# Late routing of a top-1 expert layer taken in steps inside the second products, its marks on VectorE, and the first rows' norms ahead of their transposes

## The chip, the cores and the metric

The kernel runs on one core of a Trainium2 chip. TensorE (PE) multiplies, its weight loads (PEld) overlap its products; VectorE (DVE), ScalarE (ACT) and GpSimd (POOL) compute, SyncE (SP) issues most of the transfers. The metric is the device time of one execution in microseconds; shorter is better. Three runs of the kernel before took 612.71, 613.78 and 613.82 us, median 613.78.

## What is computed

A linear attention with a norm for each head, and behind it a layer of 8 experts, of which each token goes through the one with the highest score.

```python
kv = np.einsum('bhsd,bhse->bhde', k, v)              # 8 batches, 8 heads, 576 tokens, 64
out = np.einsum('bhsd,bhde->bhse', q, kv)
rms = np.sqrt(np.mean(out * out, axis=-1, keepdims=True) + 1e-06)
x = rows_of(out / rms * g_norm)                      # 4608 tokens x 512
logits = x @ w_gate                                  # 8 experts
e_idx = np.argmax(logits, axis=1)
gate_w = softmax(logits)[np.arange(N), e_idx]
eom = 1 / (1 + np.exp(-(x @ w_output_gate)))
for e in range(8):
    mask = e_idx == e
    h = np.maximum(x[mask] @ w1[e], 0)               # 512 -> 1024
    out[mask] = gate_w[mask, None] * eom[mask, e, None] * (h @ w2[e])   # -> 512
```

## The kernel before, in words

**Early part.** `early()` goes through the first batches: `kv_part` makes the keys-values product of a batch in PSUM (`kvps`), a copy of it (`kvc`, L445, VectorE; `aug`, L446, ScalarE) is transposed and multiplied by the gate weights. `out_tile(g)` makes 128 rows of the attention (`ops`), writes them, unscaled, to a table in HBM (`xs`), and keeps squares and gate scores. The 36 tiles of 128 tokens are four groups of 10, 6, 10 and 10. For each group `route(gi)`, a generator, does the routing, nearly all of it on VectorE: the norms by a root iteration (L554 to L576, `xtail`), the scaling of the scores (L583), their sums and maximum (L587 to L600), the choice of expert (L604 to L613, `ohb`), the sums of the gates (L622 to L638); then TensorE counts each token's slot (`rps`, L641 to L650), VectorE reads it (L656 to L666), and `low` makes a 128x128 mark for each tile (`la`, L692). VectorE makes the table's right side (`rrc`, L702 to L709), writes the tail of each row (L713, L715, an SP transfer `xs<-xtail`), TensorE multiplies marks and right side (`tblps`, L724), and VectorE adds the result to `tacc` (L727, L729). The string in `PLACES` for a group says which engine makes which mark, V for VectorE and P for GpSimd, in turn.

**Order of routing.** A generator yields 0 between small operations and 1 at a pause. `advance()` takes every generator in `routing` to its next pause. `run_out` calls it after each tile, early and late; the loops at the end of `early()` and `late()` call it until nothing is left. `constant` and `constants(n)` issue 4n products of ones whose result nobody reads (L417, `cps`), called fillers below.

**Experts.** When the first 16 tiles (`EARLY`) are routed, `gather(0)` reads the first 256 rows of expert 0 with two indirect GpSimd transfers (L236, `xg`), and then `run(i)` works on one block of rows at a time: runs 0 to 7 are 256 rows of each expert, runs 8 to 15 the rest. A weight chunk (`wraw`, loaded by SP, L191) is split into two parts: ScalarE rounds it (`whi`, L211 and L218), VectorE takes the rest (`wlo`, L214 and L221). `stage(i, k)` transposes 128 gathered rows on TensorE (`tps`, L264, two PSUM buffers that are shared with `kvps`, `rps` and `tblps`) and splits them (`xT`, L267 ScalarE, L268 VectorE). `scale_heads` multiplies rows by their norms (L244): on GpSimd in `scale_rows` for every run but the first, for run 0 on VectorE inside `stage`.

The first products of a run are eight steps f of 12 products (`hps`, L289) in two PSUM buffers; of each, ScalarE makes the relu (L297) and VectorE its low part (L299, "relu half" below), after which the buffer is free for step f + 2. The second products are, for each of T tiles (T is 2 in runs 0 to 7), eight steps f of 3 products (`yps`, L326). `put(k, f, ...)` places an event behind step f of tile k: the splits of the next run's first weights, loads, the two `stage` calls of the next run and one `unit` per tile. In runs 0 to 6 a `unit` is one step of `late()`, which does the other batches, the tiles 16 to 35 and the routing of the last two groups; one unit also follows each step f of the first products. Engine orders are those of the code (`manual_schedule`): every engine executes in the order in which the instructions are issued there, and a waiting instruction holds all behind it.

## Time and profile before

| | |
|---|---|
| median of 3 runs | 613.78 us (612.71 to 613.82) |
| the profiled execution | 614.2 us, of which span 612.4 us |
| PE busy | 556.8 us (91%) |
| PEld busy | 484.0 us (79%) |
| DVE busy | 338.2 us (55%) |
| ACT busy | 285.7 us (47%) |
| POOL busy | 156.8 us (26%) |
| mean granted TensorE clock | 0.963 |

The busy shares are means over a part of some 90 us in front of run 0, a part of 240 us (runs 0 to 7, with late work beside them in runs 0 to 5), and the rest. What a stage waits for is read from the stage: from a table of busy time by stretch, from TensorE's timeline with the idle time in brackets ahead of an instruction, and from the engine that the bracket names as releaser. Times are counted from the start of the span.

### The profile page before, as it was taken

How to read it: one execution, taken by the hardware profiler on the slowest of the kernel's cores; microseconds unless marked ns; L12 is line 12 of the kernel's file. 1: busy time of each engine (PE TensorE's matmuls, PEld its weight loads, DVE VectorE, ACT ScalarE, POOL GpSimd, SP SyncE). 2: the span in 40 equal slices, each digit the busy share in tenths (PEclk: the TensorE clock that was granted, in tenths of full speed). 3: DMA queues.
4: the chain of work that ended last, by engine and by line, in shares of the span. 5: the costliest groups of instructions: out<-in, count | busy, mean ns of one | idle time of the engine just before them, and what ended most of it. 6: DMA issues, size and time to landing. Idle time of an engine off the chain costs nothing.

```text
span 612.4 us, 12185 instructions
## 1 busy us (share of the span) xinstructions
PE 556.8 (91%) x4829; PEld 484.0 (79%) x4829; DVE 338.2 (55%) x666; ACT 285.7 (47%) x481; POOL 156.8 (26%) x149
## 2 busy tenths in 40 slices
PE   7777749999999798999989999999999999999991
PEld 5656539888888687889878989889897988888980
DVE  2127846646586967765596535535445354656530
ACT  1445316658376434564544433435345453545420
POOL 2000340030301424323435216032331506050110
PEclk9989859999999988999999999999999999999996
DMA  8998966988765745776847426354453646464100
GB/s 310 406 405 329 328 235 220 371 256 311 234 244 200 246 155 161 241 210 202 276 157 238 129 103 209 121 162 165 151 185 125 218 145 207 141 217 137 42 19 17
DMA packets 43163, 125.96 MB, mean 206 GB/s; under 512 B 10302, under 2 KB 10430, under 8 KB 43104
## 3 DMA queue, kind: packets, MB, share of 16 engines
q1 hardware_dynamic: 35920, 105.19, 50.6%
q0 software_dynamic: 6752, 19.75, 9.6%
q8 instruction: 39, 0.64, 0.4%
q10 hardware_dynamic: 432, 0.22, 0.1%
q14 instruction: 20, 0.16, 0.1%
HBM read 105.94 MB, written 19.75 MB: 205 GB/s over the span
## 4 chain that ended last, share of the span: by engine, by line
PE 70%; issue 11%; DVE 6%; DMA 6%; ACT 3%; POOL 2%; another core or an unknown queue 1%; ACTq 0%; POOLq 0%; SPq 0%; DVEq 0%
PE yps L326 30%; PE hps L289 27%; PE ops L513 4%; PE tps L264 3%; PE kvps L438 3%; DMA ld<-qT 2%; DVE wlo L221 2%; DMA xg<-xs,gidx 1%; PE yps L320 1%; DMA wgs<-wg 1%; POOL out L338 1%; PE cps L417 1%; ACT whi L218 1%; DVE hT L299 1%; DMA xs<-xrow 1%
## 5 line engine op out<-in xcount | busy, mean ns | idle before, releaser
L289 PE MATMUL hps<-xT,whi 128*128 128x256 f32 (+8 forms) x1024 | 222.4, 309 | 10.1 <-DVE hT L299 8.8
L326 PE MATMUL yps<-whi,hT 128*128 128x512 f32 (+3 forms) x592 | 200.3, 402 | 0.0
L289 PEld LDWEIGHTS hps<-xT,whi 128*128 128x128 f32 x1024 | 170.7, 191 | 16.9 <-DVE hT L299 11.0
L289 PE MATMUL hps<-xT,wlo 128*128 128x256 f32 (+8 forms) x512 | 156.2, 305 | 0.0
L326 PEld LDWEIGHTS yps<-whi,hT 128*128 128x128 f32 (+3 forms) x592 | 110.8, 187 | 24.7
L338 POOL DMA_INDIRECT out<-y,oidx x42 | 45.1, 1075 | 318.0 <-ACT y L337 290.8
L299 DVE SCALAR_TENSOR_TENSOR hT<-hps,hT 128x256 fp32r<-128x256 f32 (+9 forms) x168 | 62.9, 395 | 102.8 <-ACT hT L297 94.9
L326 PE MATMUL yps<-wlo,hT 128*128 128x512 f32 (+3 forms) x296 | 116.5, 394 | 0.0
L297 ACT ACTIVATE hT<-hps 128x256 fp32r<-128x256 f32 (+8 forms) x128 | 55.4, 433 | 118.7 <-PE hps L289 113.5
L214 DVE SCALAR_TENSOR_TENSOR wlo<-wraw,gcol,whi 128x1024 fp32r<-128x1024 f32 x64 | 82.0, 1286 | 47.4 <-ACT whi L211 47.4
L289 PEld LDWEIGHTS hps<-xT,wlo 128*128 128x128 f32 x512 | 98.1, 192 | 0.3
L221 DVE TENSOR_TENSOR wlo<-wraw,whi 128x1024 fp32r<-128x1024 f32 x64 | 83.4, 1303 | 24.1 <-ACT whi L218 22.8
L211 ACT ACTIVATE whi<-wraw,gcol 128x1024 fp32r<-128x1024 f32 x64 | 72.9, 1149 | 0.0
L218 ACT CAST whi<-wraw 128x1024 fp32r<-128x1024 f32 x64 | 66.7, 1042 | 0.0
L326 PEld LDWEIGHTS yps<-wlo,hT 128*128 128x128 f32 (+3 forms) x296 | 55.6, 188 | 10.7
L244 POOL TENSOR_TENSOR xg<-xg 128x512 f32<-128x512 f32 (+8 forms) x40 | 49.4, 1240 | 33.8 <-DMA xg<-xs,gidx 32.8
L337 ACT ACTIVATE y<-yps,tl 128x512 f32<-128x512 f32 (+3 forms) x37 | 25.4, 688 | 66.5 <-PE yps L326 54.6
L236 POOL DMA_INDIRECT xg<-xs,gidx x42 | 47.0, 1118 | 16.2 <-issue 10.9
L267 ACT CAST xT<-tps 128x512 fp32r<-128x512 f32 (+8 forms) x42 | 23.0, 548 | 54.9 <-PE tps L264 53.9
L513 PE MATMUL ops<-aug,ld 64*64 64x80 f32 x1152 | 29.5, 238 | 11.1 <-DMA ld<-qT 5.1
L268 DVE TENSOR_TENSOR xT<-tps,xT 128x512 fp32r<-128x512 f32 (+8 forms) x42 | 26.7, 636 | 21.7 <-ACT xT L267 21.7
L518 ACT COPY xrow<-ops 128x512 f32<-128x512 f32 x36 | 21.3, 591 | 37.1 <-PE ops L513 28.9
(148 smaller groups left out, 405.9 us busy)
## 6 DMA issues: line engine op xcount, KB each, us to landing
wraw<-w SPq DMA_DIRECT2D x128, 512.0 KB, 4.4
ld<-kvm SPq DMA_DIRECT2D x32, 512.0 KB, 8.4
ld<-qT SPq DMA_DIRECT2D x18, 512.0 KB, 10.3
xs<-xrow SPq DMA_DIRECT2D x18, 512.0 KB, 3.6
ld<-rem SPq DMA_DIRECT2D x4, 512.0 KB, 7.5
xg<-xs,gidx POOLq DMA_INDIRECT x42
out<-y,oidx POOLq DMA_INDIRECT x42
xs<-xtail SPq DMA_DIRECT2D x3, 80.0 KB, 4.9
```

The costliest lines, as they stand in the source:

```text
L211: he.activation(hi, r, AF.Copy, scale=gcol[:, 0:1])
L214: eng.scalar_tensor_tensor(out=lo, in0=r, scalar=gcol[:, 0:1], in1=hi.bitcast(F32), op0=ALU.mult, op1=ALU.subtract)
L218: he.copy(hi, r)
L221: eng.tensor_tensor(out=lo, in0=r, in1=hi.bitcast(F32), op=ALU.subtract)
L236: nc.gpsimd.indirect_dma_start(out=x[:M, :], out_offset=None, in_=rows, in_offset=bass.IndirectOffsetOnAxis(ap=gidx[i // E][:M, p, t:t + 1 ...
L244: eng.tensor_tensor(out=v, in0=v, in1=f, op=ALU.mult)
L289: nc.tensor.matmul(ps[:, :C], w[:, o:o + P], x[d][:, :C], start=(d == 0 and k == 0), stop=(d == 3 and k == 2))
L297: nc.scalar.activation(h[:, 0:C], ps[:, :C], AF.Relu)
L299: nc.vector.scalar_tensor_tensor(out=h[:, l:l + b - a], in0=ps[:, a:b], scalar=0.0, in1=h[:, a:b].bitcast(F32), op0=ALU.max, op1=ALU.subtract)
L326: nc.tensor.matmul(ps[:M], a, b, start=(f == 0 and n == 0), stop=(f == 7 and n == 2))
L338: i_ = nc.gpsimd.indirect_dma_start(out=out, out_offset=bass.IndirectOffsetOnAxis(ap=oidx[i // E][:M, RUNS[i][0], t:t + 1], axis=0), in_=y ...
L513: nc.tensor.matmul(ps[c0:c0 + D, u, p * W:(p + 1) * W], qt[g // 2][r, p, q0:q0 + D], augs[b % 3][r, p, :], start=True, stop=True)
```

## The change

Five edits. `advance()` is called in `run_out` only while the first 16 tiles are made. A new `step(n)` takes only the oldest generator, through at most six small operations or to its next pause; the end of `late()` calls it in place of `advance()`, and in runs 0 to 7 it stands four times in each tile of the second products, behind f = 1, 3, 6 and 7. The marks of the last two groups are all made by VectorE (`PLACES`). For run 0 both tiles are scaled ahead of both `stage` calls, and 16 fillers stand in front of the first transposes, 4 in front of the second.

```diff
--- before.py
+++ after.py
@@ -64,7 +64,7 @@
 
 APART = (1, 2, 3)
 
-PLACES = ['PV', 'VVP', 'PV', 'PV']
+PLACES = ['PV', 'VVP', 'V', 'V']
 
 COLD = (2, 20, 4)
 
@@ -250,8 +250,6 @@
     def stage(i, k):
         t, c0, M = tiles_of(i)[k]
         x = xg.pop((i, t))
-        if i == 0:
-            scale_heads(x[:M], nc.vector)
         if k == 0:
             w = i // E
             n = (ROWS_A, CMAX)[w]
@@ -765,6 +763,16 @@
                 if k == 2:
                     routing.remove(r)
 
+    def step(n=6):
+
+        while n and routing:
+            n -= 1
+            k = next(routing[0], 2)
+            if k == 2:
+                routing.pop(0)
+            if k:
+                break
+
     def run_out(limit):
         nonlocal done_tiles
         if done_tiles < limit:
@@ -772,7 +780,8 @@
             done_tiles += 1
             if len(squares) > 2:
                 sums()
-            advance()
+            if done_tiles <= EARLY:
+                advance()
             return True
         return False
 
@@ -866,7 +875,7 @@
             sums()
             yield
         while routing:
-            advance()
+            step()
             yield
 
     vec = nc.vector
@@ -1029,8 +1038,11 @@
         for x in range(Tn):
             put(*places[x * len(places) // Tn], stage, i + 1, x)
         if i < E:
+
             for k in range(T):
                 put(k, 3, unit, 8 + k)
+                for f in (1, 3, 6, 7):
+                    put(k, f, step)
         order = list(range(T))
         if last_run and half(i):
             order.insert(1, order.pop())
@@ -1048,6 +1060,9 @@
         ps_y[0] = main.enter_context(tc.tile_pool(name="ps_y", bufs=1, space=psum))
         split(0, 1, 0)
         for k in range(TA):
+            scale_heads(xg[(0, k)], nc.vector)
+        for k in range(TA):
+            constants(4 if k == 0 else 1)
             stage(0, k)
         split(0, 1, 1)
         for i in range(E - 1):
```

What moves is shown for VectorE at three places. Lines of the changed kernel are up to two lower than those before for the same operation in the routing (L611 is L613).

Run 2, second products, from the split of the first weight chunk on, before:

```order
L214 SCALAR_TENSOR_TENSOR wlo<-wraw,gcol,whi 128x1024
L260 COPY tl<-xg 128x1
L268 TENSOR_TENSOR xT<-tps,xT 128x4x128
L534 TENSOR_REDUCE ss<-sq 128x8
L604 SCALAR_TENSOR_TENSOR rsc<-rd,cf 128x80
L607 TENSOR_REDUCE rsx<-rsc 128x10
L613 TENSOR_TENSOR ohb_122<-rsc,rsx 128x80
L214 SCALAR_TENSOR_TENSOR wlo<-wraw,gcol,whi 128x1024
L260 COPY tl<-xg 128x1
L268 TENSOR_TENSOR xT<-tps,xT 128x4x128
L214 SCALAR_TENSOR_TENSOR wlo<-wraw,gcol,whi 128x1024
```

and in the changed kernel, from the split of the second chunk on:

```order
L214 SCALAR_TENSOR_TENSOR wlo<-wraw,gcol,whi 128x1024
L258 COPY tl<-xg 128x1
L266 TENSOR_TENSOR xT<-tps,xT 128x4x128
L581 TENSOR_TENSOR gp<-gp,xtail 128x10x64 x2
L585 TENSOR_REDUCE lg<-gp 128x10x8
L595 TENSOR_REDUCE mx<-lg 128x10
L598 TENSOR_TENSOR rd<-lg,mx 128x80
L214 SCALAR_TENSOR_TENSOR wlo<-wraw,gcol,whi 128x1024
L602 SCALAR_TENSOR_TENSOR rsc<-rd,cf 128x80
L605 TENSOR_REDUCE rsx<-rsc 128x10
L611 TENSOR_TENSOR ohb_122<-rsc,rsx 128x80
```

The splits (`wlo`) stood with only the choice of expert (`rsc`, `rsx`, `ohb`) between them; now the scaling of the scores (`gp`), their sums and maximum stand there too, and the norms ahead of them. On TensorE the slot product `rps` of this group stood behind run 3's f = 0; it now stands behind f = 6 of run 2's last tile.

Run 4, first products, before, from the count of the last group (`cnt`) to the relu half of f = 3:

```order
L677 TENSOR_TENSOR cnt<-rps,cf 128x8
L692 TENSOR_SCALAR la<-ni,rlon 128x128 x2
L702 TENSOR_TENSOR rrc<-cf,rhk 128x10x48
L704 TENSOR_REDUCE rdn<-rex 128x10
L706 TENSOR_TENSOR rrc<-rrc,gfull 128x10x48
L707 TENSOR_SCALAR rdn<-rdn 128x10
L709 TENSOR_SCALAR rrc<-rrc,cf 128x10x48
L710 TENSOR_SCALAR rdn<-rdn 128x10
L692 TENSOR_SCALAR la<-ni,rlon 128x128 x3
L713 RECIPROCAL rdn<-rdn 128x20
L715 TENSOR_TENSOR xtail<-rdn 128x10
L299 SCALAR_TENSOR_TENSOR hT<-hps,hT 128x256
```

and in the changed kernel, from the first mark (`la`) on, with the relu halves of f = 2 and f = 3:

```order
L690 TENSOR_SCALAR la<-ni,rlon 128x128
L297 SCALAR_TENSOR_TENSOR hT<-hps,hT 128x256
L690 TENSOR_SCALAR la<-ni,rlon 128x128 x4
L700 TENSOR_TENSOR rrc<-cf,rhk 128x10x48
L702 TENSOR_REDUCE rdn<-rex 128x10
L704 TENSOR_TENSOR rrc<-rrc,gfull 128x10x48
L705 TENSOR_SCALAR rdn<-rdn 128x10
L297 SCALAR_TENSOR_TENSOR hT<-hps,hT 128x256
L221 TENSOR_TENSOR wlo<-wraw,whi 128x1024
L707 TENSOR_SCALAR rrc<-rrc,cf 128x10x48
L708 TENSOR_SCALAR rdn<-rdn 128x10
L690 TENSOR_SCALAR la<-ni,rlon 128x128 x5
```

Marks and table steps stood in one row between two relu halves; they now stand in three pieces with relu halves between, and there are ten marks on VectorE for five. The operations from `ra` to `rogs` of this group all stand in run 3's second products now.

The end of the early part, group 1 (6 tiles), before:

```order
L613 TENSOR_TENSOR ohb_124<-rsc,rsx 128x48
L727 COPY tacc<-tblps 128x96
L622 TENSOR_REDUCE ohd<-ohb_124 128x8
L625 TENSOR_TENSOR ohsum<-ohsum,ohd 128x8
L587 TENSOR_REDUCE lg<-gp 128x6x8
L633 TENSOR_TENSOR rog<-ohb_124,lg 128x48
L636 TENSOR_REDUCE rogs<-rog 128x6
L638 TENSOR_SCALAR rogs<-rogs 128x6
L445 COPY kvc<-kvps 128x256
L656 TENSOR_TENSOR rw<-rps,ohb_124 128x48
```

and in the changed kernel:

```order
L611 TENSOR_TENSOR ohb_124<-rsc,rsx 128x48
L443 COPY kvc<-kvps 128x256
L725 COPY tacc<-tblps 128x96
L620 TENSOR_REDUCE ohd<-ohb_124 128x8
L623 TENSOR_TENSOR ohsum<-ohsum,ohd 128x8
L585 TENSOR_REDUCE lg<-gp 128x6x8
L631 TENSOR_TENSOR rog<-ohb_124,lg 128x48
L634 TENSOR_REDUCE rogs<-rog 128x6
L636 TENSOR_SCALAR rogs<-rogs 128x6
L654 TENSOR_TENSOR rw<-rps,ohb_124 128x48
```

The copy of the keys-values product (`kvc`) stood behind seven operations of the routing and now stands ahead of them. At the start of run 0 VectorE's order was scale (L244), tail copy (L260), split (L268) for one tile and then the other; now the two scalings come first.

## Rows read from the trace of the kernel before

**Rows 1.** Stretches from:to, length, busy (count) PE PEld DVE ACT POOL, clock, DMA, GB/s

```profile
175.90:189.80 13.90, 13.90 (x128) 10.99 (x121) 11.79 (x25) 9.65 (x16) 1.03 (x1) 1.00 0.66 240
189.80:208.10 18.30, 15.91 (x218) 14.51 (x216) 14.34 (x38) 10.53 (x23) 7.84 (x9) 1.00 0.59 186
208.10:224.10 16.00, 13.76 (x61) 10.91 (x58) 13.18 (x24) 7.09 (x9) 2.12 (x2) 0.89 0.64 224
224.10:241.40 17.30, 14.39 (x121) 13.90 (x120) 12.70 (x34) 6.45 (x13) 9.44 (x10) 0.90 0.48 142
```

**Rows 2.** TensorE timeline: start, us, instruction, [idle before], 200 to 262 us

```profile
202.61 0.51 PE L289 MATMUL hps<-xT,whi 128*128 128x256 f32 x2 [1.68 <-DVE hT L299]
...
204.66 0.50 PE L289 MATMUL hps<-xT,whi 128*128 128x256 f32 x2 [0.36 <-DVE hT L299]
...
215.15 0.63 PE L264 MATMUL tps<-ident,xg 128*128 128x128 f32 x4 [2.24 <-issue]
...
235.06 0.50 PE L289 MATMUL hps<-xT,whi 128*128 128x256 f32 x2 [2.91 <-DVE hT L299]
...
259.87 0.50 PE L289 MATMUL hps<-xT,whi 128*128 128x256 f32 x2 [0.59 <-DVE hT L299]
```

**Rows 3.** Stretches as in rows 1, around the lower clock

```profile
216.50:219.90 3.40, 3.40 (x10) 2.66 (x9) 1.96 (x4) 1.88 (x3) 0.91 (x1) 0.56 0.47 160
...
237.00:240.40 3.40, 3.40 (x24) 3.40 (x22) 1.92 (x3) 1.30 (x3) 0.88 (x1) 0.56 0.96 349
...
83.80:93.60 9.80, 6.98 (x52) 5.63 (x52) 3.99 (x6) 3.64 (x5) 3.34 (x3) 0.52 0.86 328
```

**Rows 4.** Stretches as in rows 1, one per piece of a group's routing

```profile
159.66:161.40 1.74, 1.50 (x22) 1.20 (x20) 1.53 (x6) 0.00 (x0) 1.26 (x2) 1.00 0.54 130
167.06:167.86 0.80, 0.80 (x12) 0.74 (x7) 0.71 (x4) 0.80 (x4) 0.00 (x0) 1.00 0.96 384
172.00:173.47 1.47, 1.47 (x27) 1.34 (x29) 1.47 (x3) 1.47 (x5) 0.00 (x0) 1.00 0.69 266
175.87:177.14 1.27, 1.27 (x15) 1.07 (x10) 1.20 (x4) 1.27 (x4) 0.00 (x0) 1.00 1.02 416
181.06:181.90 0.84, 0.84 (x8) 0.68 (x6) 0.71 (x4) 0.84 (x3) 0.00 (x0) 1.00 0.23 90
187.13:189.12 1.99, 1.99 (x9) 1.59 (x9) 1.83 (x7) 1.99 (x4) 0.00 (x0) 1.00 0.64 257
197.34:198.76 1.42, 1.42 (x27) 1.33 (x19) 1.28 (x8) 1.07 (x3) 0.32 (x1) 1.00 0.05 12
199.69:202.13 2.44, 1.24 (x11) 1.03 (x9) 2.41 (x12) 1.29 (x2) 2.24 (x3) 1.00 0.38 146
```

**Rows 5.** Timeline of VectorE, then of TensorE, 70 to 89 us

```profile
70.39 0.25 DVE L727 COPY tacc<-tblps 128x96 f32<-128x96 f32 x1
...
72.57 0.42 DVE L445 COPY kvc<-kvps 128x256 f32<-128x256 f32 x1 [0.43 <-PE kvps L438]
...
76.50 1.06 PE L417 MATMUL cps<-ones 128*64 128x256 bf16 x4
...
83.80 1.09 PE L264 MATMUL tps<-ident,xg 128*128 128x128 f32 x4 [6.24 <-DVE tl L260]
...
86.89 1.11 PE L264 MATMUL tps<-ident,xg 128*128 128x128 f32 x4 [2.00 <-DVE tl L260]
...
88.68 1.30 PE L289 MATMUL hps<-xT,whi 128*128 128x256 f32 x2 [0.68 <-ACT xT L267]
```

**Rows 6.** Timeline of GpSimd, then VectorE, a scaling beside run 4's splits

```profile
234.86 3.02 POOL L244 TENSOR_TENSOR xg<-xg 128x512 f32<-128x512 f32 x2
...
234.93 2.05 DVE L221 TENSOR_TENSOR wlo<-wraw,whi 128x1024 fp32r<-128x1024 f32 x1
...
238.21 1.22 DVE L221 TENSOR_TENSOR wlo<-wraw,whi 128x1024 fp32r<-128x1024 f32 x1 [0.51 <-ACT whi L218]
```

**Rows 7.** VectorE groups by line, 156 to 242 us: xcount, busy, mean

```profile
L692 DVE TENSOR_SCALAR la<-ni,rlon 128x128 bf16<-128x128 f32 x10 | 2.3, 282 | 0.0
```

## Prediction

> **What bounds the kernel now.** I read the page first, then the stages, then the holes. By the page TensorE is the engine to watch, busy and at its full clock for most of the span after the first ninety microseconds. The table by stage [rows 1] shows where it is not the bound: run 2's second products, run 3's first and second, run 4's first, between 176 and 241 us. There VectorE is busy for 11.8 of 13.9, 14.3 of 18.3, 13.2 of 16.0 and 12.7 of 17.3 us, and in the last three TensorE has holes. The holes are listed one by one [rows 2]: 1.68 and 0.36 (run 3), 2.24 (run 3, second transposes), 2.91 (run 4), 0.59 (run 5), 7.8 us in all. Four end on VectorE's relu half (hT). The 2.24 names no releaser; by the order of the code these transposes need the PSUM buffer that VectorE frees when it has drained the table product, which stands late in its queue. In each, VectorE is in a block of routing work while TensorE waits for something short behind it. Two holes cost twice: after the 2.24 and the 2.91 the granted clock reads 0.56 for 3.4 us [rows 3], TensorE at its lower level (1.2 GHz), so 3.4 x 0.44 = 1.5 us of work is lost each time, 3.0 together. After the 1.68 it did not fall: run 3's first products stand at 1.00 [rows 1]. So this stretch holds 10.8 us.
>
> The other place is the start of run 0: from 83.8 to 93.6 us the clock is at 0.52 [rows 3]; the first transposes wait 6.24 us and start at 83.80, the second ones wait 2.00, and the first product starts at 88.68 [rows 5].
>
> **Late routing in steps.** A group's routing costs VectorE 12.0 us of stretches [rows 4]: norms 1.74, 0.80, scaling the scores 1.47, sums and maximum 1.27, choice of expert 0.84, gate sums 1.99, slots with two marks 1.42, table with three marks and tail 2.44. The steps do not shrink it; they move it out of the first products, where relu halves wait behind it, into the second, where splits do. I add up each stage.
> Run 2, second products: VectorE's 11.8 hold 4.1 of routing (1.27 + 0.84 + 1.99). Now they get 1.74 + 0.80 + 1.47 + 1.27 + 0.84 + 1.99 + 1.42 = 9.5. So 11.8 - 4.1 + 9.5 = 17.2 us of work in 13.9; 3.3 spill into run 3. TensorE's slot product moves from behind run 3's f = 0 to 0.7 us before the end of this stage, at 13.2 us, and needs the choice of expert. Ahead of that on VectorE stand 17.2 less the gate sums, the slots and one split, 12.6 us, plus up to a microsecond of waits for ScalarE: TensorE waits 0.7 (0 to 1.5).
> Run 3, first products: 14.3 hold 1.42 + 2.44 + 1.74 + 0.80 + 1.47 = 7.9 of routing; now 3.3 spilled, 2.44, and 1.0 for five more marks, 6.7. That is 13.1 in the 16.3 that the stage lasts without its holes: it fits, and 1.68 and 0.36 go. What is late next is the table product, now inside the second products, which needs ten marks, the last two behind f = 7; then the second transposes, whose PSUM buffer the first ones free; and f = 6, behind two sums of squares. I put 0.7 on each, 2.1 (0 to 3.5).
> Run 3, second products: 13.2 in 16.0, which is 12.3 without the hole and the lost clock. Routing there grows from 1.27 + 0.84 to 1.74 + 0.80 + 1.47 + 1.27 + 0.84 + 1.5 (the last group has no count to sum), from 2.1 to 7.6: 18.7 in 12.3, so 6.4 spill into run 4. There 12.7 in 17.3 (12.9 without hole and clock) hold 1.5 + 1.42 + 2.44 = 5.4; now 1.42 + 2.44 + 1.0 = 4.9 and the spill: 18.6 us in 12.9. TensorE meets 1.8 at the slot product behind f = 0 and the rest at f = 4 to 6, whose PSUM buffers the relu halves free, in pieces of 0.8 to 1.7. I take 5.5 (2.5 if two halves and a split slip into the second products, 7 with waits for ScalarE). Run 5 then finds its lists done; 0.59 goes.
> Sum: 7.8 of holes and 3.0 of clock go, 0.7 + 2.1 + 5.5 = 8.3 of holes come: 2.5 us won. None of the new holes is above 1.8, so by the 1.68 I take the clock as full.
>
> **Late marks on VectorE.** Ten late marks leave GpSimd. On VectorE one costs 2.3 us / 10 = 0.23 [rows 7]; the 2 x 5 x 0.2 = 2.0 us are in the sums above. GpSimd is freed of them, so its two scalings per run no longer wait behind marks and come earlier, beside VectorE's full stretch. Row for that: one split took 2.05 us beside GpSimd's scaling, the next 1.22 [rows 6], 0.8 more. The kernel before pays this too, so I put 0 on it, with 0 to 2.4 (three collisions) for the range. The Trainium skill, SBUF — State Buffer, section "Who interferes with whom", says that a VectorE instruction with two SBUF inputs and a GpSimd instruction that reads SBUF exclude each other, the second to issue waiting for the whole of the first; the 2.05 agrees, and by this rule every scaling that meets a split or a table step costs, which would be 3 x 0.8 and the last rival below.
> SP's tail writes of both groups now issue later in its queue, in front of weight loads of the next run; those are needed most of a stage later, and I cost them at nothing. If a split should wait for one, its weight would show as a DMA wait.
>
> **The early end.** The condition on the early tiles also ends the extra advance of early routing. On VectorE the copy of the keys-values product now stands in front of the seven operations that ran from 70.39 until the copy at 72.57, which had waited 0.43 [rows 5]. They took 2.18 - 0.43 = 1.75 us and now follow. TensorE reaches that product somewhat earlier, so the first rows' list and the gather come later by 0 to 1.75; I take 1.0. Against that, both norms now precede the transposes: at most the 2.00 us wait of the second ones is won, but four fillers stand between, 1.06 us at the lower clock [rows 5], and the second gather must have landed. I take 1.0 won: the early end is 0, from -1.0 to +1.8. The four fillers of 76.50 and the sixteen new ones take 5 x 1.06 = 5.3 us at the lower clock; begun 1.0 later, at 77.5, they end at 82.8, and the first transposes come at 84.8. That leaves 2.0 us or, at the full clock, more; an idle time like the 2.24 that preceded the lower clock, so I do not count on the full clock there.
>
> **Forecast.** The profiled execution took 614.2 us (span 612.4), 0.4 above the median of 613.8. 614.2 - 2.5 = 611.7 for a like execution, **611.3** for the median. Its own range is 609.5 to 613.0.
>
> **Rivals.** *The fillers hold the clock*: TensorE is busy 6.98 of 9.8 us from 83.8 to 93.6 at 0.52 [rows 3]; at the full clock that is 3.6, so at most 3.3 are won, 2.5 where waits for ScalarE and VectorE remain. Time 608.8. For it: the 6.24 us in front of the transposes shrink to 2 to 5. Against it: 2 stay at the least.
> *The holes close*: the spills hide in waits of VectorE for ScalarE, and run 4 has 2 us of holes instead of 5.5. Time 607. For it: VectorE is idle for a fifth of this stretch [rows 1]. Against: that idle time is spent by the sums above.
> *Nothing gained*: the sums hold but two holes come close enough together for the lower clock again: 3.0 are not won. Time 614.3.
> *Slower*: VectorE becomes the bound of run 4. Three scalings meet its full queue, 0.8 each (2.4); the holes at the slot product and at f = 4 then pass 2.2 us, the size from which the clock fell, and the 3.0 are lost as well. 2.4 + 3.0 - 2.5 = 2.9 slower, 616.7. It decides at 0.4 us more in either of these holes. The skill's rule above is this rival's ground.
>
> **Chances.** Forecast 0.45, fillers 0.12, holes close 0.08, nothing gained 0.18, slower 0.17. The bound for a difference that a measurement of this kernel can tell is about 0.2%, 1.2 us. Of the forecast's 0.45, 0.37 lies more than that below the median; with 0.12 and 0.08 faster has 0.57. Same: 0.08 and 0.17 of the fourth, 0.25. Slower 0.18. The range leaves out half of the two outer cases: 607.5 to 615.8.
>
> **What the profile of the changed kernel would show.** Right: no hole above 1.9 us between 176 and 241, granted clock 1.00 there, new waits of TensorE on VectorE's choice of expert at the end of run 2's second products and behind f = 0 of run 4, run 4's second products starting about 2 us before 241.4. The gather of the first rows about 1 us later, run 0's first product at 88 to 89. Wrong: the clock at half between 205 and 240, or one hole above 3 us in run 4 (then the spill is undercounted); a first product of run 0 before 87.5 (fillers) or after 90 (the early list costs more than the norms give).

## The result

Five runs of the changed kernel took 608.14 to 609.35 us, median **608.94**. For the kernel before the record holds five runs, the three given above and two more of 614.70 and 2990.29 us, median 613.82. The ratio of the means of the fast runs, which leaves the 2990.29 out, is 0.992 (95% interval 0.990 to 0.994); by the medians the change is 4.9 us faster. The record names no chip for either kernel here. The profiled execution took 609.33 us, its span is 607.5 us, the mean granted clock 0.976 where it was 0.963.

The five stretches of the late routing, from run 2's second products to run 4's second products, read as follows (columns as in [rows 1]: length, busy time and count of PE, PEld, DVE, ACT and POOL, granted clock, DMA share, GB/s). The first four answer to [rows 1].

```profile
173.10:187.70 14.60, 14.58 (x143) 11.38 (x135) 13.49 (x31) 9.78 (x17) 1.03 (x1) 1.00 0.62 223
187.70:203.30 15.60, 14.61 (x194) 13.59 (x193) 13.55 (x31) 10.04 (x21) 4.99 (x5) 1.00 0.72 249
203.30:216.90 13.60, 12.88 (x68) 10.12 (x67) 12.93 (x35) 7.36 (x9) 1.03 (x1) 1.00 0.57 191
216.90:235.50 18.60, 13.50 (x122) 12.63 (x120) 15.75 (x46) 6.66 (x14) 5.47 (x5) 1.00 0.39 111
235.50:247.40 11.90, 11.90 (x60) 9.84 (x57) 10.73 (x24) 7.10 (x9) 1.03 (x1) 1.00 0.84 287
```

The clock is at 1.00 throughout. Run 3 has become short; run 4's first products have become long, 18.6 us in which TensorE works 13.5. TensorE's timeline has these holes above 0.5 us there (idle time in the bracket, then its releaser), and ahead of them the slot product of run 2, which has none; they answer to [rows 2].

```profile
186.62 0.41 PE L646 MATMUL rps<-ohb,ones 128*128 128x80 bf16 x10
...
200.31 0.51 PE L287 MATMUL hps<-xT,whi 128*128 128x256 f32 x2 [0.72 <-DVE hT L297]
...
209.62 0.63 PE L262 MATMUL tps<-ident,xg 128*128 128x128 f32 x4 [0.65 <-issue]
...
220.31 0.41 PE L646 MATMUL rps<-ohb,ones 128*128 128x80 bf16 x10 [1.66 <-DVE ohb L611]
...
227.09 0.50 PE L287 MATMUL hps<-xT,whi 128*128 128x256 f32 x2 [1.83 <-DVE hT L297]
...
229.30 0.50 PE L287 MATMUL hps<-xT,whi 128*128 128x256 f32 x2 [0.53 <-DVE hT L297]
...
232.07 0.50 PE L287 MATMUL hps<-xT,whi 128*128 128x256 f32 x2 [1.08 <-DVE hT L297]
```

At the early end the fillers, the transposes and the first product stand at these times; they answer to the last rows of [rows 5]. The stretch from 84.2 to 93.5 us is at a clock of 0.52, as it was in [rows 3].

```profile
77.05 2.37 PE L415 MATMUL cps<-ones 128*64 128x256 bf16 x20
...
84.26 1.12 PE L262 MATMUL tps<-ident,xg 128*128 128x128 f32 x4 [4.84 <-DVE xg L244]
...
86.69 1.11 PE L262 MATMUL tps<-ident,xg 128*128 128x128 f32 x4 [0.32 <-DVE tl L258]
...
88.47 1.30 PE L287 MATMUL hps<-xT,whi 128*128 128x256 f32 x2 [0.67 <-ACT xT L265]
```

From the first product to the last, the start of every stage against the kernel before gives where the 4.9 us between the two profiles lie: 0.1 up to run 0's second products; **2.7 in runs 1 and 2 ahead of the late routing** (46.94 to 45.86 us, 19.43 to 17.80); **3.5 from run 2's second products to run 5's** (89.78 to 86.27); then 0.6 given back in run 7's first products and 0.9 in runs 12 and 13. The 2.7 us are new to the prediction. Of them 2.2 stand in two keys-values products, one in each run, which take 2.23 and 2.27 us for 1.15 and have pauses of TensorE in them with no releaser (0.60 and 0.64 us of idle time; the products around them are slower too). The other 0.5 stand in run 2 behind these, without a hole that the profile marks. Here is the product of run 1 in the kernel before, TensorE's timeline:

```profile
127.25 0.57 PE L438 MATMUL kvps<-ld 128*64 128x64 f32 x12
128.07 0.39 PE L438 MATMUL kvps<-ld 128*64 128x64 f32 x5 [0.25 <-issue]
128.81 0.68 PE L438 MATMUL kvps<-ld 128*64 128x64 f32 x15 [0.35 <-issue]
```

and the same 32 products in the changed one, in one row:

```profile
127.15 1.15 PE L436 MATMUL kvps<-ld 128*64 128x64 f32 x32
```

### The profile page after: what moved, and what is told of

It is laid out like the page before. It is cut to its first block, busy times and chain, and to the rows that moved or that the text cites. A ratio compares the mean times of both kernels' runs of the same rounds, so it can differ in the third digit from the quotient of the medians.

```text
span 607.5 us, 12239 instructions
## 1 busy us (share of the span) xinstructions
PE 557.1 (92%) x4857; PEld 483.9 (80%) x4857; DVE 341.1 (56%) x676; ACT 286.3 (47%) x481; POOL 148.7 (24%) x139
## 4 chain that ended last, share of the span: by engine, by line
PE 70%; issue 10%; DVE 8%; DMA 5%; ACT 2%; POOL 2%; ACTq 0%; POOLq 0%; SPq 0%; DVEq 0%
PE yps L324 29%; PE hps L287 27%; PE ops L511 4%; PE kvps L436 3%; PE tps L262 3%; DMA ld<-qT 2%; DVE wlo L221 2%; DMA xg<-xs,gidx 2%; PE yps L318 1%; POOL out L336 1%; DMA wgs<-wg 1%; ACT whi L218 1%; PE cps L415 1%; DVE hT L297 1%; DVE la L690 1%
## 5 line engine op out<-in xcount | busy, mean ns | idle before, releaser
L244 POOL TENSOR_TENSOR xg<-xg 128x512 f32<-128x512 f32 (+8 forms) x40 | 48.1, 1206 | 45.7 <-DMA xg<-xs,gidx 45.3
L511 PEld LDWEIGHTS ops<-aug,ld 64*64 64x64 f32 x1152 | 23.9, 136 | 17.1 <-issue 11.9
```

Source lines behind the costliest of these rows:

```text
L244: eng.tensor_tensor(out=v, in0=v, in1=f, op=ALU.mult)
L511: nc.tensor.matmul(ps[c0:c0 + D, u, p * W:(p + 1) * W], qt[g // 2][r, p, q0:q0 + D], augs[b % 3][r, p, :], start=True, stop=True)
```

## The experiments

Each comparison below ran on one chip, with runs of the kernel before among them. The four comparisons, e1 to e4, e5 to e8, e9 to e11, and e12, used four chips. Lengths of stages in the table are from the first product of a stage to the first of the next, in us, in one profiled execution each; "late" is the sum from run 2's second to run 5's first products.

| kernel | median, kernel before | ratio (95%) | run 2, 1st | run 2, 2nd | run 3, 1st | run 3, 2nd | run 4, 1st | run 4, 2nd | run 5, 1st | late | run 7, 1st |
|---|---|---|---|---|---|---|---|---|---|---|---|
| before | 613.82 | | 19.43 | 13.88 | 18.25 | 16.01 | 17.43 | 11.87 | 12.34 | 89.78 | 14.94 |
| after | 608.94, 613.82 | 0.992 (0.990 to 0.994) | 17.80 | 14.59 | 15.59 | 13.63 | 18.55 | 11.95 | 11.96 | 86.27 | 15.55 |
| e1 steps | 612.52, 612.69 | 1.000 (0.998 to 1.003) | 18.07 | 14.59 | 15.58 | 13.16 | 20.34 | 11.87 | 11.95 | 87.49 | 14.56 |
| e2 marks | 614.85, 612.69 | 1.004 (1.002 to 1.006) | 18.09 | 13.89 | 19.45 | 13.54 | 19.28 | 11.87 | 12.35 | 90.38 | 14.96 |
| e3 norms | 613.14, 612.69 | 1.000 (0.997 to 1.002) | 17.80 | 13.89 | 18.23 | 15.95 | 17.13 | 11.88 | 12.34 | 89.42 | 16.21 |
| e4 hole | 611.16, 612.69 | 0.998 (0.996 to 1.001) | 17.79 | 14.60 | 15.59 | 14.07 | 19.41 | 11.96 | 11.95 | 87.58 | 14.94 |
| e5 after again | 610.15, 612.47 | 0.996 (0.994 to 0.998) | 17.80 | 14.60 | 15.82 | 13.50 | 18.45 | 11.95 | 11.96 | 86.28 | 15.10 |
| e6 spread | 605.88, 612.47 | 0.988 (0.986 to 0.991) | 17.81 | 13.88 | 15.79 | 12.39 | 12.06 | 14.78 | 13.53 | 82.43 | 14.96 |
| e7 list | 607.50, 612.47 | 0.991 (0.989 to 0.994) | 17.80 | 14.59 | 15.59 | 13.51 | 18.58 | 11.96 | 11.95 | 86.18 | 12.47 |
| e8 fill | 608.40, 612.47 | 0.994 (0.991 to 0.996) | 17.80 | 14.59 | 15.57 | 13.55 | 18.53 | 11.95 | 11.94 | 86.13 | 15.86 |
| e9 before again | 613.88 (one run) | | 19.30 | 13.89 | 18.25 | 15.84 | 16.38 | 11.87 | 12.36 | 88.59 | 14.30 |
| e10 all three | 608.76, 615.53 | 0.988 (0.986 to 0.991) | 18.92 | 13.89 | 17.20 | 12.39 | 12.06 | 14.77 | 13.35 | 83.66 | 12.71 |
| e11 fine | 610.82, 615.53 | 0.993 (0.991 to 0.995) | 19.24 | 15.14 | 17.28 | 13.79 | 13.14 | 14.42 | 12.02 | 85.79 | 12.81 |
| e12 two | 610.34, 614.24 | 0.992 (0.989 to 0.995) | 19.09 | 13.89 | 17.15 | 13.30 | 16.36 | 13.72 | 12.78 | 87.20 | 12.82 |

### The steps alone

The changed kernel without its marks and its norms:

```diff
-PLACES = ['PV', 'VVP', 'V', 'V']
+PLACES = ['PV', 'VVP', 'PV', 'PV']
...
+        if i == 0:
+            scale_heads(x[:M], nc.vector)
...
-            scale_heads(xg[(0, k)], nc.vector)
-        for k in range(TA):
-            constants(4 if k == 0 else 1)
```

> The steps alone: late marks half on GpSimd and the first rows' norms as in the kernel before. Queue theory (the time went because VectorE's routing block was cut up, and what is left is VectorE's work in runs 3 and 4): the steps carry the late gain alone, and with 5 marks of 0.23 us less in each group VectorE's run 4 is 1.1 us shorter than in the changed kernel; about 608 us, full clock from 200 to 240 us, holes of 4 us in run 4 instead of 5.1. Rival (marks): on GpSimd they stand behind its scalings of 3 us, so the table product waits for them, and the steps alone bring less than 1 us: 613. For the keys-values products of runs 1 and 2, 2.2 us each before and 1.1 in the changed kernel: if the 20 fillers in front of run 0 are what shifted them, they take 2.2 us here.

612.52 against 612.69 us: no gain that can be measured, where 608 was expected. By the trace the steps do what they should in run 3 (15.58 and 13.16 us) and the clock stays at 1.00, but run 4's first products take 20.34 us. The holes there are 1.66, 1.39, 0.89, 0.71 and one that the changed kernel does not have; TensorE's timeline:

```profile
237.02 0.26 PE L724 MATMUL tblps<-rrc,la 128*128 128x96 bf16 x2 [1.98 <-POOL la L692]
```

GpSimd's timeline ahead of it:

```profile
230.97 2.43 POOL L692 TENSOR_SCALAR la<-ni,rlon 128x128 bf16<-128x128 f32 x3
233.37 2.03 POOL L244 TENSOR_TENSOR xg<-xg 128x512 f32<-128x512 f32 x2
235.39 1.57 POOL L692 TENSOR_SCALAR la<-ni,rlon 128x128 bf16<-128x128 f32 x1
```

In pieces, the marks reach GpSimd on both sides of its next scaling, and the last one ends 2 us late for the table product. The rival's mechanism is there, at its price. What does not fit is the sum: against the norms alone, on the same chip, the late part of this trace is 1.9 us shorter, and the medians show 0.6, with intervals of about 1.5 to either side. The profiled execution, 610.74 us, was also faster than the median. So the gain that the trace has in the late part is not shown by the runs.

### The marks alone

```diff
-PLACES = ['PV', 'VVP', 'PV', 'PV']
+PLACES = ['PV', 'VVP', 'V', 'V']
```

> The late marks on VectorE alone, routing in the long stretches of before, norms as before. Queue theory: each late group puts 5 x 0.23 = 1.15 us more in front of a relu half, the holes of 1.68 and 2.91 us grow by that, 613.8 + 2.3 = 616.1 us (614.5 to 616.5), and the half clock after the larger ones stays. Rival (marks on GpSimd held the table product): 1 to 2 us faster, 612 to 613. Keys-values products of runs 1 and 2 at 2.2 us each, if the fillers are what shifted them.

Slower by 0.4%, 2.5 us by the ratio, where 2.3 were expected. The two holes of [rows 2] with five more marks in front of their relu halves are 2.87 (0.73 and 2.14) for 1.68, and 4.58 for 2.91, which is 1.2 and 1.7 us more for the 1.15 that was expected of each. TensorE's timeline:

```profile
203.47 0.51 PE L289 MATMUL hps<-xT,whi 128*128 128x256 f32 x2 [2.14 <-DVE hT L299]
...
234.90 0.80 PE L289 MATMUL hps<-xT,whi 128*128 128x256 f32 x2 [4.58 <-DVE hT L299]
```

Ahead of the second the first five marks, beside a scaling of 1.04 us on GpSimd that starts at 230.00, took 0.8 us more than the last five (VectorE's timeline):

```profile
229.84 1.87 DVE L692 TENSOR_SCALAR la<-ni,rlon 128x128 bf16<-128x128 f32 x5
...
233.06 1.06 DVE L692 TENSOR_SCALAR la<-ni,rlon 128x128 bf16<-128x128 f32 x5
```

The half clock did not stay after both, as was expected: behind the 2.14 us it is at 1.00. The hole of 2.24 in the second transposes is 1.38 here, without a fall of the clock, and so the late part of this profile is only 1.0 us longer than that of the norms alone on the same chip; the rest of the 2.5 us is not located. So the late marks are a loss of 0.4% by themselves. On top of the steps they come with a gain: the late part is 86.27 us for 87.49, and the ratio goes from 1.000 to 0.996, but on two chips and with the norms added; on the chip of the steps alone, the kernel of e4 below, which has marks and norms and a longer hole, is 1.4 us below them by the medians, hardly more than the noise. The 1.98 us wait for GpSimd only exists once the routing is in pieces.

### The norms and fillers alone

```diff
-        if i == 0:
-            scale_heads(x[:M], nc.vector)
...
+            scale_heads(xg[(0, k)], nc.vector)
+        for k in range(TA):
+            constants(4 if k == 0 else 1)
```

> Both norms in front of the first transposes and the 16 + 4 fillers alone; late routing and marks as before. Theory of the prediction: the first product of run 0 within 0.5 us of 88.7, nothing else moves, 613.8 us within 0.5. Rival (fillers shift TensorE's instructions): the keys-values products of runs 1 and 2 take 1.1 us each instead of 2.2 and run 3 starts 2 to 2.7 us earlier, 611.1 us.

No difference, as the prediction had it. The rival falls with it: the keys-values products of runs 1 and 2 take 1.15 us each here, but also in the two kernels above, which have no fillers. So the fillers do not decide on these pauses. One part of the expectation failed: run 0's first product stands at 89.90 us, not within 0.5 of 88.7. A single profile cannot show a move of that size: the changed kernel had it at 88.47 and, in its second profile, at 90.48, and e5 and e7, whose early parts are the same and which ran on one chip, at 90.48 and 88.28.

Run 7's first products are the longest of all kernels here, 16.21 us. TensorE's timeline has this hole there, and behind it the clock is at the lower level (stretch):

```profile
311.32 0.50 PE L287 MATMUL hps<-xT,whi 128*128 128x256 f32 x2 [1.76 <-DVE hT L297]
```

```profile
312.60:316.00 3.40, 3.40 (x17) 3.37 (x16) 1.92 (x7) 0.51 (x2) 0.00 (x0) 0.51 0.00 1
```

A fall behind 1.76 us: the prediction had taken the clock as full behind holes up to 1.8 us, from one hole of 1.68.

### A longer hole in run 4

```diff
+    late_wait = c1.tile([P, P], F32, name="late_wait")
...
             unit(f)
+            if i == 4 and f == 1:
+                for x in range(4):
+                    nc.vector.tensor_scalar(out=late_wait, in0=cf[:, 0:P], scalar1=1.0, scalar2=None, op0=ALU.add)
```

> The changed kernel with four more VectorE operations on 128x128 (0.28 us each, 1.1 together) behind run 4's f = 1, in front of the relu half for which TensorE has its hole of 1.83 us. Theory (a hole above 2.2 us brings the half clock): the hole becomes 2.9, and the granted clock falls to about 0.56 for 3.4 us, 1.1 + 1.5 = 2.6 us slower than the changed kernel, 611.5. Rival (clock not tied to one hole): 1.1 slower, 610.0, clock at 1.00. Rival (slack): the spill is taken up behind it, within 0.3 of 608.9.

In TensorE's timeline the hole of 1.83 us is now

```profile
229.88 0.51 PE L287 MATMUL hps<-xT,whi 128*128 128x256 f32 x2 [2.68 <-DVE hT L297]
```

and behind it the granted clock falls (stretch, columns as in [rows 1]):

```profile
231.00:234.40 3.40, 3.12 (x16) 2.82 (x15) 3.40 (x14) 0.39 (x1) 0.00 (x0) 0.52 0.00 0
```

The clock went as the theory said, the price did not: run 4's first products take 19.41 instead of 18.45 to 18.55 us, 0.9 more and not 2.6. The later holes of 0.53 and 1.08 us have shrunk to 0.28 and nothing. Here VectorE was the bound, and the work that TensorE lost was taken from its own later waits. The median is 1.0 us above that of the changed kernel, taken on another chip, so it does not tell the three expectations apart; the reading rests on the trace.

### The changed kernel again

The same kernel, on another chip than in the first comparison.

> The changed kernel once more, beside the kernel before on the same chip. From the start of run 2's second products to the start of run 5 the kernel before took 77.4 us (77.1 with the norms alone), the changed one 74.3, and run 5's first products 0.4 less. Theory (only this is the change; the pauses in the keys-values products of runs 1 and 2, 2.7 us together, were in the one profiled execution of before and in none of four others): 3.5 us, a ratio of 0.994, and 74.3 within 0.3 in the trace. Rival (the 4.8 us of the first comparison are all of the change): 0.992.

The ratio is 0.996 (0.994 to 0.998), 2.3 us by the medians; the interval does not meet that of the first comparison, so the rival is out. The theory's 0.994 lies at its edge: the runs show less than the 3.5 us that the traces have in the late part. That part is 86.28 us, the same as in the first profile of the changed kernel within 0.01; the kernel before was not profiled in this comparison. So the change is worth about 2.3 us here, and 4.9 us there.

### The kernel before again

> The kernel before, once more, for a second profile of it. Theory (the pauses of TensorE in the keys-values products of runs 1 and 2, 1.1 and 1.6 us, belonged to one execution): from run 0's second products to run 2's first 45.9 us instead of 46.9, run 2's first products 17.8 instead of 19.4. Rival (they belong to the kernel before): 46.9 and 19.4 again. In either case 77.1 to 77.5 us from run 2's second products to run 5, with the half clock after holes of 2.2 and 2.9 us.

The rival was right: 47.04 and 19.30 us, the pauses are there again.

```profile
127.52 0.56 PE L438 MATMUL kvps<-ld 128*64 128x64 f32 x10
128.39 0.35 PE L438 MATMUL kvps<-ld 128*64 128x64 f32 x5 [0.31 <-issue]
129.15 0.70 PE L438 MATMUL kvps<-ld 128*64 128x64 f32 x17 [0.40 <-issue]
```

But they do not belong to the kernel before alone. The two other kernels of the same comparison (e10 and e11: 18.92 and 19.24 us for run 2's first products) have them as well, and so has the last one, on yet another chip (19.09); all eight kernels of the other two chips have none. They go with the chip, or with something that held for the whole of a comparison. The medians of the kernel before agree: 615.53 and 614.24 us where the profiles have the pauses, 612.69 and 612.47 where they have none. In the first pair of profiles the kernel before had them and the changed one had not. That is 2.7 us, or 0.44%, and it is just what separates 0.992 from 0.996; whether the other runs were of the same kind no profile shows, nor whether the two kernels ran on the same chip there.

This second profile also shows that what the clock costs is less sure than I took it. TensorE's holes are as in [rows 2]:

```profile
215.21 0.63 PE L264 MATMUL tps<-ident,xg 128*128 128x128 f32 x4 [2.05 <-issue]
...
235.24 0.50 PE L289 MATMUL hps<-xT,whi 128*128 128x256 f32 x2 [2.91 <-DVE hT L299]
```

and the stretches behind them:

```profile
216.50:219.90 3.40, 3.40 (x10) 2.63 (x9) 2.20 (x5) 2.05 (x3) 1.07 (x1) 0.51 0.42 147
236.50:239.90 3.40, 3.22 (x33) 3.03 (x32) 2.76 (x5) 1.70 (x3) 1.56 (x1) 1.00 1.00 295
```

After 2.05 us the clock falls, after 2.91 it does not, where in the first profile of the same kernel it fell after both. The late part is 88.59 us here, 1.2 less than in the first profile, and 1.05 of that in run 4's first products (16.38 for 17.43 us), the stage with the same hole of 2.91 and without the fall: that is what the fall cost there, where the prediction took 1.5.

### Smaller portions

```diff
         while routing:
-            step()
+            step(1)
             yield
...
                 for f in (1, 3, 6, 7):
-                    put(k, f, step)
+                    put(k, f, step, 4)
```

> The changed kernel with smaller portions: one routing operation behind each f of the first products instead of six, four in each step of the second products instead of six. The last group's routing then ends in run 5's second products instead of run 4's. Theory (run 4's holes of 1.66, 1.83, 0.53 and 1.08 us are VectorE's backlog there, and runs 5 and 6 have room: 6.2 of 12.0 us busy): holes of run 4 fall from 5.1 to 1.5 us, 3.5 us faster than the changed kernel. Rival (the slot products and the table product wait for VectorE wherever they are put): the same holes at other places, within 1 us of the changed kernel.

605.88 us, 4.3 below the changed kernel on the same chip, 0.988 of the kernel before. Run 4's first products take 12.06 us instead of 18.45. Some comes back behind them, 2.8 us in run 4's second products and 1.6 in run 5's first, of which this wait is the largest (TensorE's timeline):

```profile
238.82 0.41 PE L646 MATMUL rps<-ohb,ones 128*128 128x80 bf16 x10 [2.19 <-DVE ohb L611]
```

So both had a part right: the slot product waits wherever VectorE has a backlog, but a backlog that is moved to a stage with room is mostly gone. The clock is at 1.00 behind these 2.19 us.

### The list of overflow blocks

```diff
-            run(i, lambda n: next(listing, None))
+            run(i, lambda n: next(listing, None) if i >= E else None)
```

> The changed kernel with the list of overflow blocks begun in run 8's first products instead of run 7's. Run 7's first products take 14.6 to 16.2 us in the six traces so far, run 6's 12.0 with the same products. Theory (the list's small operations in front of relu halves make run 7's holes of 3 us): run 7's first products take 12.2 us, 3 us faster than the changed kernel. Rival (GpSimd's scaling of four blocks, which meets the splits there, makes them): 14 us, at most 1 us faster.

Run 7's first products take 12.47 us as the theory said, 2.6 less, and the median falls by 2.65. The list does cost something where it stands now: from run 7's second products to run 12's first it is 162.39 us instead of 160.68, with one hole of 1.48 us, which ends on ScalarE's split. So the stages that the list touches give 0.9 us net in these two profiles; where the rest of the 2.65 comes from stays open. On the changed kernel the list also shows one reason why run 7's length wanders (14.3 to 16.2 us in the table). VectorE's timeline there:

```profile
301.50 1.06 DVE L949 TENSOR_TENSOR flew<-perm,cf 128x64 f32<-128x64 f32 x1
...
303.06 1.77 DVE L960 TENSOR_SCALAR cnp<-cnt 128x8 f32<-128x8 f32 x1
```

and GpSimd's beside it:

```profile
300.83 1.65 POOL L244 TENSOR_TENSOR xg<-xg 128x512 f32<-128x512 f32 x1 [0.33 <-DMA xg<-xs,gidx]
302.66 1.06 POOL L336 DMA_INDIRECT out<-y,oidx  x1 [0.18 <-issue]
303.74 1.06 POOL L244 TENSOR_TENSOR xg<-xg 52x512 f32<-52x512 f32 x1
```

Clear of GpSimd the same two operations took 0.27 and 0.16 us in this experiment. TensorE's hole of 2.21 us in the changed kernel ends on the relu half behind the first of them, one of 0.74 us on that behind the second. Another reason is the clock: in the two longest of these stages, 16.21 us (e3) and 15.86 (e8), it fell, behind holes of 1.76 and 2.17 us; with the changed kernel's 2.21 it did not.

### More fillers

```diff
-            constants(4 if k == 0 else 1)
+            constants(12 if k == 0 else 1)
```

> The changed kernel with 48 fillers in front of the first transposes instead of 16. In its trace the fillers ran at the full clock, 0.47 us for four, and behind them TensorE stood idle for 4.84 us until the first transposes; 32 more take 3.8 us at the full clock, 7.6 at the lower one. Theory (the idle time is what brings the half clock that lasts from 84 to 93.5 us): the first transposes and run 0's first steps are at 1.00, run 0 is 2.5 us shorter, 2.5 us faster. Rival (the clock falls in any case, the fillers at half clock reach past the moment at which the scaled rows are there): transposes up to 3 us later, 0 to 3 us slower.

Here the fillers reach up to the transposes (TensorE's timeline), and the clock is full behind them (stretch):

```profile
78.11 7.19 PE L415 MATMUL cps<-ones 128*64 128x256 bf16 x52
85.25 0.66 PE L262 MATMUL tps<-ident,xg 128*128 128x128 f32 x4
```

```profile
88.00:92.00 4.00, 2.99 (x45) 2.56 (x44) 2.50 (x5) 2.54 (x4) 1.50 (x1) 1.00 1.03 401
```

Run 0's first products take 19.23 us instead of 20.99, and the median is 1.75 us lower. The theory holds for this execution, at two thirds of the price. Of the other nine runs no profile tells whether the clock held, and it is not sure to happen: in the three kernels below, with the same fillers, they ran at the full clock all along (5.87 us for the same 52 in the next one), ended earlier and left 1.4 us in front of the transposes, and the clock from 88 to 92 us was 0.50 again.

### The three together, and two finer ways

> The three earlier edits together on the changed kernel: one and four routing operations at a time, the list from run 8 on, 48 fillers. If the three gains are at different places and do not meet (run 4 and 5; run 7; run 0), they add: 4.3 + 2.6 + 1.7 = 8.6 us below the changed kernel's 610.2, 601.5 us. Rival (what is won in one place is waited for at the next, above all loads of weights that then come late): 604 or more.

0.988 of the kernel before, and no more than the smaller portions alone. The theory's 601.5 us is out, the rival's 604 or more came. Run 4 and run 7 kept their gains (12.06 and 12.71 us); run 0 did not (21.26 us, the clock at 0.50), run 3's first products are 1.4 us longer than with the smaller portions alone (17.20 for 15.79, with longer waits for ScalarE and VectorE, as in the two kernels below), and some of the list's gain came back behind. That these waits are for late weights, as the rival had it, is not shown. The chips differ as well, this one with the pauses in runs 1 and 2, so 608.76 is not to be set against 605.88; the two ratios are.

The next takes two operations at each of eight steps of a tile in the second products, with the rest as in the three together.

```diff
-                for f in (1, 3, 6, 7):
-                    put(k, f, step, 4)
+                for f in range(8):
+                    put(k, f, step, 2)
```

> As the kernel with the three edits, but two routing operations behind each of the eight steps of a tile in the second products instead of four behind four of them. By the order the choice of expert then stands before run 4's second products, so the slot product behind it should not wait (2.2 us with four operations), and the scaling of the scores stands in run 4's first products. Theory: run 4's second products take 12.5 instead of 14.8 us, 2 us below the kernel with the three edits, 599.5. Rival (VectorE's work is the same and the wait only moves into run 4's first products): within 0.7 us of it.

Slower than the three together by 0.45%, 2.1 us by the medians on the same chip, so neither came true. The slot product waits no longer in run 4 and 0.58 us in run 2, but all that there was to win in run 4's second products is 0.35 us, and the stages ahead of it are longer: 15.14, 13.79 and 13.14 us for run 2's second, run 3's second and run 4's first products, where the three together took 13.89, 12.39 and 12.06.

The last takes two operations behind each f of the first products, with the rest as in the three together.

```diff
         while routing:
-            step(1)
+            step(2)
             yield
```

> As the kernel with the three edits, but two routing operations behind each f of the first products instead of one. By the order the choice of expert of the last group then stands behind run 4's f = 7, ahead of the second products in which TensorE counts slots; with one operation it stood behind two splits and the scaling of the scores there, and TensorE waited 2.2 us. Theory: that wait goes, run 4's second products take 12.5 us instead of 14.8 and its first products 12.1 to 12.8, 1.5 to 2 us below the kernel with the three edits, a ratio of 0.9855 to the kernel before. Rival (run 4's first products, with 5 us of routing in them again, take over the wait): run 4 as a whole within 0.5 us of it, 0.988.

0.992, and the rival's way, beyond its size: the slot product does not wait in run 4's second products, which are 1.05 us shorter, and run 4's first products are 4.3 us longer, so run 4 as a whole is 3.3 us longer and not within 0.5. VectorE's timeline has the scaling of the scores there, which meets GpSimd's scaling of rows:

```profile
228.08 3.25 DVE L581 TENSOR_TENSOR gp<-gp,xtail 128x640 f32<-128x640 f32 x2
```

```profile
227.05 3.60 POOL L244 TENSOR_TENSOR xg<-xg 128x512 f32<-128x512 f32 x2 [2.69 <-DMA xg<-xs,gidx]
```

In the kernel with smaller portions the same two took 1.55 us. A relu half stands behind them, TensorE waits 2.42 us for it (TensorE's timeline), and the clock falls (stretch):

```profile
231.72 0.51 PE L287 MATMUL hps<-xT,whi 128*128 128x256 f32 x2 [2.42 <-DVE hT L297]
```

```profile
233.00:236.40 3.40, 3.40 (x17) 3.33 (x16) 1.99 (x5) 0.55 (x2) 0.00 (x0) 0.50 0.37 113
```

This is the prediction's slowest rival, a scaling, a hole above 2.2 us and a fall of the clock, in a kernel that took smaller steps than the changed one.

## Why the prediction was right, and where it was not

611.3 us, 607.5 to 615.8, faster: the time of 608.94 lies in it, and the direction held. Step by step:

- **What bounds the kernel.** Right. VectorE's routing in front of relu halves made the holes; moving it moved them (e1, e6, e12), and putting marks in front of them lengthened them by 1.2 and 1.7 us for 1.15 us of marks (e2).
- **Run 2, second products.** 0.7 us of wait for the slot product was expected. There is none: its row at 186.62 us has no bracket. The stage is 0.71 longer, as it now holds the product itself.
- **Run 3.** 2.1 us were expected, 0.7 at each of three places. Two of them came, 0.72 and 0.65; the table product did not wait.
- **Run 4.** 5.5 us were expected, 1.8 at the slot product and the rest in pieces of 0.8 to 1.7. 5.10 came: 1.66, then 1.83, 0.53 and 1.08. The places are those of the forecast, behind f = 0 and at f = 4 to 6, so the walk through VectorE's queue was right almost to the step. The amount of work was not: VectorE was busy for 15.75 us of the 18.60, where the sum put 18.6 us of work there and no waits, so that the total came so close is partly luck.
- **The sum of the late part.** Holes of 7.8 us were to become 8.3 and 3.0 us of lost clock to go, 2.5 won. From run 2's second to run 5's first products TensorE's idle time went from 8.1 to 7.0 us and its busy time from 81.7 to 79.3, 3.5 won: the term of the new holes was some 1.8 too large (6.5 for 8.3), that of the clock 0.6 too large. Set against the second profile of the kernel before, where the clock fell once, it is 2.3.
- **The rule that a hole of 2.2 us decides on the clock.** The step that failed, though the time did not hang on it. The clock fell after 1.76 in one profile (e3) and 2.05 in another, stayed after 2.91 in that same one (e9), stayed after 2.14 (e2) and 2.19 (e6) and fell after 2.42 (e12) and 2.68 (e4). A long hole makes it likely, its length alone does not settle it. That the clock stayed full behind the new holes, of up to 1.83 us, was therefore partly luck. The price of 1.5 us a time was not fixed either: the fall in run 4 of the kernel before cost 1.05 us, set against its second profile, and e4 paid next to nothing for its fall, in a stage that VectorE bounds.
- **The marks at no cost beyond the sums.** Right for the pair of edits, and for a reason that the prediction had only half: without them the table product waits 1.98 us for GpSimd (e1). Alone they cost 2.5 us (e2). Of the three collisions with scalings that the slowest rival priced at 0.8 us each none came: from run 2's second to run 4's first products no split took more than 1.38 us. One of its kind came in e12.
- **The early end at 0.** Not refuted: the first product moved by 0.2 us between the first two profiles and the norms alone measure as nothing (e3), but the changed kernel's own second profile has it at 90.48, beyond the 90 that was named as a sign of a dearer list. Since the same early part gave 88.28 as well (e7), that sign could not decide anything in one profile. That the fillers would not hold the clock was right; they ran faster than was counted, twenty in 2.37 us for 5.3, and left 4.84 us in front of the transposes instead of 2.0. With 48 for the 16 the clock held in one profile of four (e8).
- **What was not in it.** The 2.7 us in runs 1 and 2, which kernels with and without the change have on two chips and none has on two others, and 1.5 given back in runs 7, 12 and 13. Run 7's stand beside the meetings of its list with GpSimd; those of run 12 recur: its first products took 14.72 us in the five profiles without the whole change and 15.03 to 15.36 in the nine with it, for a reason that I did not follow up. On the chip of the repeat the change gave 2.3 us, the size that was forecast; that the first result was 4.9 lies, as far as the profiles tell, in the pauses. They are also about the 2.4 us by which the measured time lies below the forecast.

Of the versions tried, smaller portions behind the first products are the best, 0.988 of the kernel before alone and with the two other edits, against 0.992 and 0.996 for the changed kernel.

## What to carry to other kernels

Cutting a block of side work into pieces pays when the pieces land in stages where their engine has room, so add up each stage's work on that engine first: one or two operations behind each step of the first products made run 4's first products take 12.06 or 16.36 us here. An edit's worth can change sign with its neighbour (the marks: 0.4% lost alone; with the steps a wait of 1.98 us gone, and the runs, on two chips, on the side of a gain), so judge a bundle's parts also in pairs. And before a gain of some tenths of a per cent is put down to a change, look in the traces for a difference in stages that the change does not touch, and repeat both kernels on another chip.

## What the runs showed of the hardware

- TensorE's pauses of 0.23 to 0.41 us in two keys-values products, without a releaser, came in every kernel of two comparisons and in none of two others, each on its own chip. What causes them stays open; the fillers ahead of them do not decide it, since kernels with and without fillers are on both sides.
- The granted clock's fall behind a hole is not the same in two executions of one kernel (1.00 and 0.56 behind 2.91 us), and it came behind a hole as short as 1.76 us (0.51).
- A GpSimd scaling holds up even small VectorE operations: beside one of 128x512, one on 128x64 took 1.06 us instead of 0.27; beside a transfer's issue and a scaling of 52x512, one on 128x8 took 1.77 instead of 0.16 (rows under the list of overflow blocks). A late mark, with one tensor and one value for each partition as inputs, took 1.07 us in this row of VectorE's timeline of the kernel with smaller portions, beside a scaling of 128x512 at 251.44, where its neighbours took 0.27:

```profile
252.41 1.07 DVE L690 TENSOR_SCALAR la<-ni,rlon 128x128 bf16<-128x128 f32 x1
...
253.74 0.27 DVE L690 TENSOR_SCALAR la<-ni,rlon 128x128 bf16<-128x128 f32 x1
```

The Trainium skill, SBUF — State Buffer, section "Who interferes with whom", counts `tensor_scalar` among the operations that can contend with GpSimd for the ports they share, where its operands allow a mode that uses both ports, besides operations with two SBUF inputs; the row agrees.
